# An attention and gated-MLP kernel: score slots, side matmuls and PSUM banks shared between them, and the last block divided on chip

## The chip, the cores and the metric

The kernel runs on one core of a Trainium2 chip. The metric is the device time of one execution in microseconds (us). Every changed kernel here ran four times, with the kernel before beside it on the same chip. Ratios to the kernel before use fast executions alone; medians are over all. The profiled execution of each kernel gives its span, its waits and the clock granted to TensorE (1.0 is full speed). PE is TensorE, PEld its weight loads, DVE VectorE, ACT ScalarE, POOL GpSimd, SP SyncE. "L416" is line 416 of the kernel in question; the line numbers shift a little from one kernel to the next.

## The reference

```python
x  = A_x                                  # 1 x 2048 x 640, bf16
xn = layernorm(x)
q, k, v = split(xn @ wqkv)                # 32 heads of 20
s  = softmax(q @ k.T * 20**-0.5) @ v @ wo
g  = silu((sigmoid(xn @ w_gate) * (xn @ w_up)) @ w_down)   # inner size 1728
return x + s * g
```

The heads are taken four at a time (the four 32-row strips of TensorE's array) and the queries 512 at a time, which makes 8 x 4 = 32 blocks.

## The kernel before

The kernel plans its own issue order. While it is built, a small planner walks through time in steps, holds a model of when each engine is free, and emits one instruction after the other. The chip then executes each engine's list in exactly that order. What waits for what is not the planner's work: the program builder puts in the semaphore waits.

Scores of one key tile and head fill one PSUM bank (128 x 512 fp32). Most are turned into probabilities by an exp on ScalarE, two or three banks in one instruction. Some key tiles go to VectorE, which makes the exponential with integer arithmetic (`iv`, then four passes `pb`). All other matmuls, projections and the MLP, are "side work". These tiles take eight banks of PSUM, the memory that TensorE writes its results to:

```python
SLOT = (3, 2)
scA = [psum.tile([P, n, 512], FP32, name=f"scA{n}", tag=f"scA{n}") for n in SLOT]  # 3 + 2 banks
scD = psum.tile([P, 512], FP32, name="scD", tag="scD")      # scores for VectorE
oacc = psum.tile([P, QC], FP32, name="oacc", tag="oacc")    # sum of values
def misc_ps():                                              # every side matmul
    return psum.tile([P, 512], FP32, tag="misc", bufs=1, name="mps")
...
# ScalarE: one exp over all banks of a slot
exp_act(pt[:, 0:m, :], scA[i][:, 0:m, :])
...
# VectorE: one bank
nc.vector.tensor_scalar(out=d["iv"][:, j, :], in0=scD, scalar1=I_OFF, scalar2=I_LOW, ...)
...
# TensorE: a fill of the slot that is free, plus one head for VectorE, packed side by side
todo = [(scA[nfill % 2][:, x, :],) + t for x, t in enumerate(jobs)]
...; todo.append((scD, dcur["b"], dcur["kt"], js[0]))
```

The packed score matmuls that write a slot are called its fill. A side item, for example a gate tile, takes the one side bank, runs its five matmuls, waits for ScalarE or VectorE to read the bank, and only then gives it to the next.

Of the kernel before, what the change touches and what calls it, by code (L numbers as in the profile page):

```python
# [10 lines left out]
FP32 = mybir.dt.float32  # L11
# [3 lines left out]
ALU = mybir.AluOpType  # L15
# [11 lines left out]
ND = 4  # L27

# [22 lines left out]
def kernel(  # L51
# [50 lines left out]
    ident = const.tile([P, P], BF16, name="ident")  # L102
    esum = const.tile([P, P], BF16, name="esum")
# [30 lines left out]
    mks = {}  # L134
# [8 lines left out]
    def k_max(g, c):  # L143
        if c == 0:
            mks[g] = wk.tile([P, NQC], FP32, tag="mk4", bufs=2, name="mk4")
        nc.vector.tensor_reduce(out=mks[g][:, c:c + 1], in_=kTs[g % 2][:, c * 512:(c + 1) * 512],
                                axis=AXISX, op=ALU.max, apply_absolute_value=True)
        if c == NQC - 1:
            mk = wk.tile([P, 1], FP32, tag="mk", bufs=2, name="mk")
            nc.vector.tensor_reduce(out=mk, in_=mks[g], axis=AXISX, op=ALU.max)  # L150
            nc.vector.tensor_scalar_mul(out=mds[g % 2], in0=esum, scalar1=mk[:, 0:1])
# [41 lines left out]
    with tc.tile_pool(name="ln", bufs=2) as lp, \  # L193
# [10 lines left out]
        make_identity(nc, ident)  # L204
        for w in wqks:
            nc.gpsimd.memset(w.rearrange("p a j e -> p (a j e)"), 0.0)
# [18 lines left out]
        for c in range(NQC):  # L225
# [16 lines left out]
            for i in range(4):  # L242
                if i % 2 == 0:
                    nc.scalar.activation(out=xn[:, i, :], in_=xt[:, i, :], func=ACT.Identity,
                                         bias=nb[:, i, :], scale=rstd[:, i, :])
                else:
                    nc.gpsimd.tensor_scalar(out=xn[:, i, :], in0=xt[:, i, :], scalar1=rstd[:, i, :],
                                            scalar2=nb[:, i, :], op0=ALU.mult, op1=ALU.add)
            for kd in range(KD):
# [5 lines left out]
                if kd % 2 == 0:  # L255
                    nc.scalar.copy(out=dst, in_=tp)
                else:
                    nc.vector.tensor_copy(out=dst, in_=tp)
# [17 lines left out]
    SLOT = (3, 2)  # L276
    scA = [psum.tile([P, n, 512], FP32, name=f"scA{n}", tag=f"scA{n}") for n in SLOT]
    scD = psum.tile([P, 512], FP32, name="scD", tag="scD")
# [3 lines left out]

    def misc_ps():
        return psum.tile([P, 512], FP32, tag="misc", bufs=1, name="mps")
# [19 lines left out]
    LAT = 0.07  # L304
    D_WAIT = 0.0
    T_F, T_PV, T_MM, T_MODE = 0.215, 0.216, 0.216, 0.10
    T_IV, T_PASS, T_ON = 0.655, 0.63, 0.66
    NPT, NPB, NIV = (3, 4), 2, 2

    def t_exp(n):  # L310
        return 0.095 + 0.4267 * n
# [8 lines left out]

    class Item:
        def __init__(self, ops, at, need=None, prio=1):
            self.ops = ops
            self.at = at
            self.need = need
            self.prio = prio
            self.i = 0
            self.ready = 0.0

    def mk_k(g, c, at):  # L330
        st = {}

        def alloc():
# [4 lines left out]
                     ("DVE", 0.66, lambda: k_max(g, c))], at, prio=0)  # L338
# [5 lines left out]
    def mk_q(b, at):  # L344
# [13 lines left out]
        def ev():  # L358
            qs[b] = q_evac(st["ps"])
        return Item([("PE", alloc, [(T_MM, lambda kd=kd: mm(kd)) for kd in range(KD)]),  # L360
                     ("ACT", 0.53, ab),
                     ("PE", None, [(T_MM, lambda: q_bound(st["ps"], g, st["aq"]))]),
                     ("DVE", 0.66, ev, "free", lambda t: q_at.__setitem__(b, t))], at, prio=0)

    def mk_v(pr, tts, at):
# [10 lines left out]
        def done(t):  # L376
            for tt in tts:
                v_at[(pr, tt)] = t + (2.5 if tt in DKT else 0.0)
        nd = sum(tt in DKT for tt in tts)
        return Item([("PE", alloc, [(0.07, lambda i=i, kd=kd: mm(i, kd)) for i in range(len(tts)) for kd in range(KD)]),  # L380
                     ("DVE", 0.1 + 0.18 * len(tts) + 0.28 * nd, lambda: v_evac(st["ps"], pr, tts), "free", done)], at, prio=0)

    def mk_gu(c, kf, at):
# [25 lines left out]
        def ev():  # L409
# [3 lines left out]
                      ("ACT", 0.53, th, "free")], at),  # L413
                Item([("PE", alloc1, [(T_MM, lambda kd=kd: mm("u", 1, kd)) for kd in range(KD)]),
                      ("DVE", 0.66, ev, "free")], at)]

    def mk_down(c, t4, h, at):
# [15 lines left out]
        def ev():  # L433
# [4 lines left out]
        return Item([("PE", alloc, [(0.136, lambda kf=kf: mm(kf)) for kf in range(NFT)]),  # L438
                     ("ACT", 0.37, th), ("DVE", 0.44, ev, "free")], at)

    def mk_out(tt, h, at):
        st = {}

        def alloc():
            if h == 0:
                if not ob:
                    ob.append(late.tile([P, 2, 5 * D], BF16, name="ob", tag="wd"))
                o2 = ob[0][:, tt % 2, :]
                xr, ot = o2[:, 0:D], o2[:, D:2 * D]
                gqr = o2[:, 2 * D:4 * D].bitcast(FP32)  # L450
                nc.sync.dma_start(out=xr, in_=x2[tt * P:(tt + 1) * P, :])
                nc.sync.dma_start(out=gqr, in_=gq_dram[tt * P:(tt + 1) * P, :])
                out_tiles[tt] = (xr, gqr, ot)
            st["ps"] = misc_ps()
# [5 lines left out]
        def ev():  # L460
            xr, gqr, ot = out_tiles[tt]
            sl = slice(h * HD, (h + 1) * HD)
            tmp = ob[0][:, h, 4 * D:5 * D].bitcast(FP32)
# [3 lines left out]
            if h == 1:  # L467
                nc.sync.dma_start(out=out2[tt * P:(tt + 1) * P, :], in_=ot)
        return Item([("PE", alloc, [(0.136, lambda kd=kd: mm(kd)) for kd in range(KD)]),
                     ("DVE", 0.44, ev, "free")], at, need=(NG - 1) * NQC + tt // 4)  # L470
# [9 lines left out]
    nglu = NBLK - NQC  # L480
    gi = 0
    items = [mk_v(0, t, 0.0) for t in VT]
    for b in range(NBLK):
# [7 lines left out]
        if b < nglu:  # L491
            hi = (len(glu) * (b + 1)) // nglu
            mk += glu[gi:hi]
            gi = hi
        elif c > 0:
# [5 lines left out]
        for i, f in enumerate(mk):  # L501
            items += f(b + 0.9 * i / len(mk))

# [3 lines left out]
    claimed = [0]  # L507

    def claim_act(n):
        got = []  # L510
        for b in range(min(NBLK - 1, claimed[0] // NJOB), NBLK):
# [16 lines left out]
    def claim_dve():  # L528
        for b in range(claimed[0] // NJOB, min(NBLK, claimed[0] // NJOB + 2)):
            if d_left[b]:  # L530
# [4 lines left out]
            if a_left[b]:  # L535
                return None
# [12 lines left out]
    pt_left = [[], []]  # L549
# [17 lines left out]
    def pv_emit(us, end):  # L567
        for u in us:
# [15 lines left out]
            left[i][1] = max(left[i][1], end + LAT)  # L584
# [42 lines left out]

    with tc.manual_schedule(engines={ENG.PE, ENG.Activation, ENG.DVE}):
        nc.sync.dma_start(out=wo, in_=A_wo.rearrange("(kd p) e -> p kd e", p=P))
        load_wgu(0, 0)  # L630
# [7 lines left out]
        slots = [dict(full=None, at=0.0), dict(full=None, at=0.0)]  # L638
        nfill, nexp = 0, 0
        dslot = dict(full=None, at=0.0)  # L640
        iv_left = []
        dcur = None
        dve_pass = []
        cur = None
        mode = None
        blk_loaded = -1
        misc_at = 0.0
        extra = []
        norm_pending = None
        STEP = 0.04  # L650

        def progress():
            return claimed[0] / NJOB

        def finish(item, t):
            op = item.ops[item.i]
            item.i += 1
            item.ready = t + LAT
# [3 lines left out]
        while pv_block[0] < NBLK:  # L662
            guard += 1
            assert guard < 60000, ("issue order does not end", now, claimed, pv_block, [len(q) for q in pv_q], slots, dslot, cur and (cur.i, cur.ops[cur.i][0], cur.ready), misc_at, items[:1] and (items[0].at, items[0].need), [(u["b"],u["kt"],u["k"],u["ready"]) for u in pv_q[0][:3]], [(u["b"],u["kt"],u["k"],u["ready"]) for u in pv_q[1][:3]], pt_left[0][-4:], pt_left[1][-4:], pb_left[-3:], iv_left[-3:], dcur and dcur["left"], oacc_at, norm_pending, sorted(v_at)[-3:])
            bb = min(NBLK - 1, claimed[0] // NJOB)
# [7 lines left out]
            if cur is None and misc_at <= now:  # L673
                can = [x for x in items[:80] if x.at <= progress() and (
                    x.need is None or o_at.get(x.need, 1e9) <= now)]
                cur = min(can, key=lambda x: x.prio) if can else None
            if cur is not None and cur in items:
                items.remove(cur)
                cur.ready = now
                step = 0  # L680
            for it in list(extra):
                if it.i >= len(it.ops):
                    extra.remove(it)
            evs = ([cur] if cur is not None else []) + extra


            if free["ACT"] <= now:
                it = next((e for e in evs if e.i < len(e.ops) and e.ops[e.i][0] == "ACT" and e.ready <= now), None)
                s = slots[nexp % 2]
                if it is not None:  # L690
                    op = it.ops[it.i]
                    op[2]()
                    free["ACT"] = now + op[1]
                    finish(it, now + op[1])
                    if len(op) > 3 and op[3] == "free":
                        misc_at = now + op[1] + LAT
                        if it is cur:
                            cur = None
                            if it.i < len(it.ops):
                                extra.append(it)  # L700
                elif s["full"] is not None and s["at"] <= now and buf_free(pt_left[nexp % 2], NPT[nexp % 2]):
                    jobs = s["full"]
                    i = nexp % 2
                    pt = w2.tile([P, SLOT[i], QC], BF16, tag=f"pt{i}", bufs=NPT[i], name=f"pt{i}")
                    m = len(jobs)
                    exp_act(pt[:, 0:m, :], scA[i][:, 0:m, :])
                    end = now + t_exp(m)
                    free["ACT"] = end
                    pt_left[i].append([m, 0.0])
                    for x, (b, kt, j) in enumerate(jobs):  # L710
                        add_unit(b, kt, j, pt[:, x, :], None, end + LAT + 0.1, (pt_left[i], len(pt_left[i]) - 1))
# [209 lines left out]
```

## Time and profile before

The time was 976.27 us (median of 3; 975.0 to 977.9). The profiled execution has a span of 963.7 us. Its own device time was 965.4 us, at a clock of 0.981.

| stage | from, to (us) | what limits it |
|---|---|---|
| head (normalise, transpose, first keys) | 0 to 39.2 | PE waits 18 us for normalised rows |
| attention (first to end of last exp) | 39.2 to 866.8, 827.5 us | ScalarE, closely followed by TensorE |
| tail (last down projections, output) | 866.8 to 963.7, 96.9 us | one PSUM bank, used in turn |

The first lines of the page of the kernel before. Each digit of the middle rows is the busy share of one fortieth of the span, in tenths; PEclk is the granted clock.

```profile
span 963.7 us, 18399 instructions
...
PE 867.8 (90%) x7285; PEld 306.8 (32%) x7372; DVE 768.1 (80%) x1302; ACT 802.9 (83%) x790; POOL 107.3 (11%) x152
...
PE   3799999999999999999999999999999999997664
...
ACT  3769998989999898979999999999999899981000
...
PEclk9799999999999999999999999999999999998889
```

In the attention TensorE is at 9 throughout; ScalarE, from the fourth slice on, is mostly at 9 and else at 8 (once at 7). ScalarE drops to 1 and then to nothing in the last four slices, where TensorE goes on at 7 to 4: that is the tail.

Busy times overlap, so headroom is read from starts. In this timeline of ScalarE (start, duration, what) a three-bank exp (128x1536) is followed 1.33 us later by the next instruction, and a two-bank exp (128x1024) 0.91 us later when nothing is waited for (303.08 to 303.99). After the exp at 300.72 the next one starts 1.02 us later: the other slot was filled late.

```profile
299.39 1.56 ACT L81 ACTIVATE pt_3820<-scA_428 128x1536 bf16<-128x1536 f32 x1
300.72 1.14 ACT L81 ACTIVATE pt_3838<-scA_429 128x1024 bf16<-128x1024 f32 x1
301.74 1.47 ACT L81 ACTIVATE pt_3848<-scA_428 128x1536 bf16<-128x1536 f32 x1
303.08 1.04 ACT L81 ACTIVATE pt_3862<-scA_429 128x1024 bf16<-128x1024 f32 x1
303.99 1.48 ACT L81 ACTIVATE pt_3875<-scA_428 128x1536 bf16<-128x1536 f32 x1
```

By such distances ScalarE needs an estimated 649 of the 700 us between 100 and 800 (93%).

The tail, in the chain of waits (start, duration, what): each down projection (14 matmuls) is followed by a tanh, a multiplication on VectorE, and only then by the next one.

```profile
883.73 2.18 PE mps L425 x14
...
885.93 0.45 ACT td L81
...
886.40 0.50 DVE gqs L435
...
886.95 2.18 PE mps L425 x14
```

Two groups of the view by lines serve for comparison. The columns are: line, engine, operation, out<-in, shapes, count, then busy us and mean ns of one, then idle us just before them with what ended it.

```profile
L747 DVE TENSOR_SCALAR iv<-scD 128x512 int16<-128x512 f32 x452 | 310.0, 686 | 95.4 <-PE scD L540 85.9 <-PE scA_429 L540 5.8 <-PE scA_428 L540 1.5
...
L402 PE MATMUL mps<-xnT,wgu 128*128 128x512 bf16 x465 | 138.4, 383 | 5.6 <-issue 1.3 <-DVE q L168 0.8 <-DVE vf L184 0.8
```

Side matmuls of the MLP hardly ever wait (5.6 us before 465 of them).

### The profile page before, as it was taken

What the parts mean: (1) busy time and instruction counts of PE and PEld (TensorE: products, weight loads), DVE (VectorE), ACT (ScalarE), POOL (GpSimd) and SP (SyncE); (2) the same over time, 40 slices, a digit from 0 to 9 for tenths busy, and PEclk for the clock granted to TensorE, in tenths of its full rate; (3) what the DMA queues carried; (4) which work ended last, traced back from release to release, by engine and by line L of the source; (5) the groups of instructions that cost most, each with busy time, mean ns of one, the idle gap of its engine ahead of it and who ended that gap; (6) DMA issues with size and microseconds to landing.
All of it is one profiled execution on the core that took longest, in us unless ns stands there. A gap on an engine that the chain in (4) does not pass through costs nothing.

```text
span 963.7 us, 18399 instructions
## 1 busy us (share of the span) xinstructions
PE 867.8 (90%) x7285; PEld 306.8 (32%) x7372; DVE 768.1 (80%) x1302; ACT 802.9 (83%) x790; POOL 107.3 (11%) x152
## 2 busy tenths in 40 slices
PE   3799999999999999999999999999999999997664
PEld 1333323333333233332333333333233322223332
DVE  6588889898888888888888889898888888883122
ACT  3769998989999898979999999999999899981000
POOL 4110010110001000100000000110000000000044
PEclk9799999999999999999999999999999999998889
DMA  8301211112110211111110111102121111211366
GB/s 215 126 10 43 49 44 33 47 48 53 30 38 29 52 44 41 45 42 46 45 42 20 41 33 44 44 16 64 44 58 30 38 50 45 62 44 31 109 185 184
DMA packets 85798, 54.53 MB, mean 57 GB/s; under 512 B 33552, under 2 KB 79440, under 8 KB 85712
## 3 DMA queue, kind: packets, MB, share of 16 engines
q1 hardware_dynamic: 84560, 52.05, 19.7%
q8 instruction: 57, 0.93, 0.4%
q10 hardware_dynamic: 1152, 1.31, 0.4%
q14 instruction: 29, 0.24, 0.1%
HBM read 42.32 MB, written 8.39 MB: 53 GB/s over the span
## 4 chain that ended last, share of the span: by engine, by line
PE 49%; ACT 24%; DVE 18%; issue 5%; DMA 3%; POOL 1%; SPq 0%; POOLq 0%; DVEq 0%; another core or an unknown queue 0%; ACTq 0%
PE oacc L580 13%; PE mps L402 10%; DVE pb L625 7%; PE scA_428 L540 6%; PE mps L425 5%; DVE iv L747 5%; PE scA_429 L540 5%; PE scD L540 4%; PE mps L457 2%; PE mps L372 2%; PE mps L341 1%; DVE ob L464 1%; PE mps L352 1%; DMA ob<-gq_dram 1%; DVE hT L410 1%
## 5 line engine op out<-in xcount | busy, mean ns | idle before, releaser
L747 DVE TENSOR_SCALAR iv<-scD 128x512 int16<-128x512 f32 x452 | 310.0, 686 | 95.4 <-PE scD L540 85.9
L625 DVE TENSOR_SCALAR pb<-iv 128x2048 int16<-128x2048 int16 x452 | 307.9, 714 | 3.0
L402 PE MATMUL mps<-xnT,wgu 128*128 128x512 bf16 (+1 forms) x505 | 150.9, 385 | 7.7 <-DVE hT L410 1.4
L610 POOL TENSOR_TENSOR on_bf<-on,rl 128x512 bf16<-128x512 f32 x32 | 42.7, 1335 | 558.0 <-DMA rl<-rd 341.6
L540 PE MATMUL scD<-q,kT_69 32*128 32x512 bf16 x228 | 87.9, 385 | 2.3 <-DVE iv L747 1.8
L425 PE MATMUL mps<-wd,hT 128*128 128x320 bf16 x448 | 80.9, 306 | 8.6 <-DVE gqs L435 7.5
L540 PE MATMUL scD<-q,kT_70 32*128 32x512 bf16 x224 | 85.6, 382 | 2.1 <-DVE iv L747 1.8
L580 PE MATMUL oacc<-pb,vs_74 128*21 128x512 bf16 x684 | 80.2, 382 | 1.7 <-DVE pb L625 1.2
L580 PE MATMUL oacc<-pb,vs_73 128*21 128x512 bf16 x672 | 79.7, 382 | 1.6 <-DVE pb L625 1.3
L540 PEld LDWEIGHTS <-kT_70 32*128 32x128 bf16 x1024 | 38.5, 91 | 123.4 <-issue 119.4
L540 PEld LDWEIGHTS <-kT_69 32*128 32x128 bf16 x1024 | 39.2, 91 | 120.8 <-issue 113.9
L402 PEld LDWEIGHTS <-wgu 128*128 128x128 bf16 (+1 forms) x560 | 44.1, 98 | 85.1 <-issue 58.4
L540 PE MATMUL scA_428<-q,kT_69 32*128 32x512 bf16 x478 | 64.5, 387 | 7.4 <-DVE q L168 3.2
L540 PE MATMUL scA_428<-q,kT_70 32*128 32x512 bf16 x480 | 64.8, 383 | 4.6 <-ACT pt_2941 L81 0.5
L540 PE MATMUL scA_429<-q,kT_70 32*128 32x512 bf16 x320 | 64.0, 383 | 1.4 <-ACT pt_3070 L81 0.4
L540 PE MATMUL scA_429<-q,kT_69 32*128 32x512 bf16 x318 | 63.3, 386 | 1.4 <-ACT pt_7252 L81 0.5
L425 PEld LDWEIGHTS <-hT 128*128 128x128 bf16 x448 | 38.9, 98 | 49.4 <-issue 37.4
L457 PE MATMUL mps<-wo,oU 128*128 128x320 bf16 x160 | 31.2, 332 | 23.1 <-DVE ob L464 22.1
L464 DVE SCALAR_TENSOR_TENSOR ob<-mps,ob 128x320 f32<-128x320 f32 x32 | 15.7, 492 | 38.2 <-PE mps L457 31.1
L81 ACT ACTIVATE tnh<-mps 128x512 bf16<-128x512 f32 (+1 forms) x56 | 35.6, 636 | 10.5 <-PE mps L402 10.5
L410 DVE SCALAR_TENSOR_TENSOR hT<-tnh,mps 128x512 bf16<-128x512 bf16 (+1 forms) x56 | 38.1, 681 | 4.4 <-PE mps L402 3.9
L580 PEld LDWEIGHTS <-v_71 128*21 128x21 bf16 x1024 | 27.7, 90 | 41.1 <-issue 33.0
(1374 smaller groups left out, 1754.5 us busy)
## 6 DMA issues: line engine op xcount, KB each, us to landing
rl<-rd SPq DMA_DIRECT2D x128, 64.0 KB
wgu<-in_B_w_gate_dram SPq DMA_DIRECT2D x24, 320.0 KB
wgu<-in_B_w_up_dram SPq DMA_DIRECT2D x24, 320.0 KB
gq_dram<-gqs SPq DMA_DIRECT2D x32, 160.0 KB
ob<-gq_dram SPq DMA_DIRECT2D x16, 320.0 KB
ob<-in_A_x_dram SPq DMA_DIRECT2D x16, 160.0 KB
out_dram<-ob SPq DMA_DIRECT2D x16, 160.0 KB
oU<-on_bf SPq DMA_DIRECT2D x112, 20.0 KB
```

Of the source, the lines that this page charges most:

```text
L81: return nc.scalar.add_instruction(mybir.InstActivation(func=func, name=nc.get_next_instruction_name(), engine=ENG.Activation, ins=[nc.sca ...
L372: nc.tensor.matmul(st["ps"][:, i * 2 * GC:(i + 1) * 2 * GC], lhsT=xnT[:, kd, tts[i] * P:(tts[i] + 1) * P], rhs=wvs[pr][:, kd, :], start=(k ...
L402: nc.tensor.matmul(st[key][0:fs, :], lhsT=w[:, i, kd, ko * P:ko * P + fs], rhs=xnT[:, kd, c * QC:(c + 1) * QC], start=(kd == 0), stop=(kd ...
L410: nc.vector.scalar_tensor_tensor(out=hT[0:fs, kf, :], in0=st["t"][0:fs, :], scalar=1.0, in1=st["u"][0:fs, :], op0=ALU.add, op1=ALU.mult)
L425: nc.tensor.matmul(st["ps"][:, 0:HD], lhsT=hT[0:fsz[kf], kf, t4 * P:(t4 + 1) * P], rhs=wd[0:fsz[kf], kf, h * HD:(h + 1) * HD], start=(kf = ...
L457: nc.tensor.matmul(st["ps"][:, 0:HD], lhsT=oU[:, kd, tt * P:(tt + 1) * P], rhs=wo[:, kd, h * HD:(h + 1) * HD], start=(kd == 0), stop=(kd = ...
L464: nc.vector.scalar_tensor_tensor(out=tmp, in0=st["ps"][:, 0:HD], scalar=0.25, in1=gqr[:, sl], op0=ALU.mult, op1=ALU.mult)
L540: nc.tensor.matmul(dst, lhsT=kTs[(b // NQC) % 2][32 * j:32 * j + 32, kt * P:(kt + 1) * P], rhs=qs[b][32 * j:32 * j + 32, :], start=True, s ...
L580: nc.tensor.matmul(oacc[32 * j:32 * j + DH + 1, :], lhsT=lhsT, rhs=u["src"], start=first, stop=last, tile_position=(0, 32 * j), skip_group ...
L610: nc.gpsimd.tensor_tensor(out=on_bf, in0=on, in1=rl, op=ALU.mult)
L625: nc.vector.tensor_scalar(out=pb[:, k, :, :].bitcast(I16), in0=iv, scalar1=0.25, scalar2=cst, op0=ALU.mult, op1=ALU.add)
L747: nc.vector.tensor_scalar(out=d["iv"][:, j, :], in0=scD, scalar1=I_OFF, scalar2=I_LOW, op0=ALU.add, op1=ALU.max)
```

## The change

The intent: two score slots of three banks each, of which the third bank is not the slot's own. Together with the bank `mps` these third banks are a pool of three from which an exp, a VectorE score or a side item takes whichever is free. Side work is paced so that it is done when the attention ends. The last block is divided on chip, by transposes, instead of by a trip through DRAM. The head normalises on VectorE.

```diff
-    SLOT = (3, 2)
-    scA = [psum.tile([P, n, 512], FP32, name=f"scA{n}", tag=f"scA{n}") for n in SLOT]
-    scD = psum.tile([P, 512], FP32, name="scD", tag="scD")
+    SLOT = 3
+    scA = [psum.tile([P, SLOT, 512], FP32, name=f"scA{i}", tag=f"scA{i}") for i in range(2)]
...
+    mps = psum.tile([P, 512], FP32, name="mps", tag="mps")
+    bank = [scA[0][:, SLOT - 1, :], scA[1][:, SLOT - 1, :], mps]
+    got_bank = [2]
     def misc_ps():
-        return psum.tile([P, 512], FP32, tag="misc", bufs=1, name="mps")
+        return bank[got_bank[0]]
...
+        def due():     # side work that should be done by now
+            return total * min(1.0, progress() / (NBLK - NQC - 0.2))
...
+                        behind = done < due() + LAG
+                        for f in ((2, (nfill + 1) % 2, nfill % 2) if behind else (2,)):
+                            if flex[f] <= now:
+                                m_bank = f
...
+                    want = SLOT if flex[nfill % 2] <= now and d_bank != nfill % 2 else SLOT - 1
+                    jobs = claim_act(want)
...
+                            score_mm(bank[d_bank], dcur["b"], dcur["kt"], d_new[1])
... (new constants of the planner, items that wait for named events, tail_steps() for the last block,
...  normalisation on VectorE, copies of xnT on ScalarE)
```

## The prediction

> **What bounds it now.** Span 963.7 us, three stages (slices, chain of waits, timeline):
> - Head: the first score matmul starts at 38.75. PE waits 18 us for normalised rows (ScalarE 13.5, GpSimd 4.4).
> - Attention: exps run from 39.2 to 866.8, 827 us for 32 blocks. From 100 to 800 PE is busy 96%, ACT 95%, DVE 87%, but busy times overlap. By start-to-start times ScalarE is tightest: a 3-bank exp takes 1.33, a 2-bank one 0.905, tanh and abs 0.478; it needs 649 of 700 us (93%). 40 of the 51 lost come after the 2-bank exp (mean 1.062): the other slot is filled late. TensorE rounds take 0.22 (four packed matmuls), 0.216 (side), 0.136 (320 columns), plus 0.10 at each change of kind. The Trainium skill, "TensorEngine Tiling (Array Packing)", Key Properties, says that changing the tiling mode drains the engine; the trace agrees (0.32 against 0.216). By the issue order this makes 753 us, 91% of its stage.
> - Tail: 97 us. Eight down projections and 32 output halves share one PSUM bank strictly in turn (3.2 and 1.5 us each), with DMA waits of 3 to 4 us; PE is half idle and its clock falls to 0.5 in places ("TensorE: Matmul & The Clock Gate", Part 1: an idle window throttles it).
>
> **What the change does** (issue order of both).
> - Tail: all downs and 15 halves move into attention. 9 halves remain (about 13 us), then the last block, divided on chip: copy, transposes, 40-odd matmuls, VectorE, output DMA (about 14). Estimate 29 us after the last exp, for 97: minus 68.
> - Head: normalising goes to VectorE (16 ops of about 0.3), all xnT copies to ScalarE: minus 4.
> - Attention: TensorE gets downs (15 us), halves (10), 725 fill rounds for 684; floor 789 for 753. Changes of kind hardly fall (1547 for 1563). ScalarE: 559 2-bank and 166 3-bank exps for 319 and 319, 20 score tiles more: 778 for about 762. VectorE needs about 675, no limit. Against that, side work runs in three banks without its serial wait, and VectorE tiles queue. At ScalarE's old 93% the stage would take 838, at 97% 802. But two engines now need 95% at once, and in most rounds a fill (about 0.7 with latencies) must fit within 0.905, so I expect 94 to 95%: 826 us, as long as before.
>
> **Sum.** 35 + 826 + 29 = 890 us profiled. Timed runs before were 11 above the profiled one (976 for 965), so about 899; I say 896, range 870 to 928. Chances: faster by over 2% 0.94, within 2% 0.05, slower 0.01. The gain comes from tail and head; attention absorbs 36 us of TensorE work at no cost in time.
>
> **What would show it.** Tail: last exp to end about 29 us (right under 36); no chain of down projection, tanh, VectorE. Head: first score near 35, no wait of PE for GpSimd. Attention: exps last about 826; ScalarE's idle per exp falls to about 0.06 (0.157 after 2-bank exps before); VectorE's waits for the score bank (86 us) halve. PE clock 1.0 throughout attention.
>
> **What would make it wrong.** If each 2-bank exp still loses 0.157, attention takes 866 and the time is 935. If the planned order fits the chip's durations very well, 805 and 875. Output halves waiting for rows from DRAM, or for the reciprocal's trip through DRAM, could add 5 to 10 to the tail. If flexible banks make a fill wait for a slow VectorE read, ScalarE starves, as at block changes (waits up to 5 us before).

## The result

The changed kernel takes 1287.56 us (median of 4; 1282.5 to 1300.0) against 975.63 for the kernel before (972.1 to 977.9): 1.322 times as long, with a 95% interval of 1.311 to 1.333. (Ratios are the mean time of one kernel's fast runs over that of the other's of the same rounds, so not quite the ratio of the medians.) Executions over 1.5% slower than the fastest of the same kernel are left out of the means. The output is correct.

The page after:

```profile
span 1298.2 us, 18464 instructions
...
PE 998.7 (77%) x7243; PEld 306.1 (24%) x7328; DVE 757.5 (58%) x1272; ACT 862.8 (66%) x876; POOL 95.3 (7%) x138
...
PE   4777778887877787787887777787877777787775
...
ACT  5567676765556777666678867666657765786760
...
PEclk8589898986678989787799989888879997999888
```

No engine is at 9 anywhere. TensorE, at 7 or 8, is busier in sum than before (998.7 us for 867.8) though it has no more matmuls to do; the clock fell to half in places (0.50 from 40 to 60 us, mean 0.871), and matmuls take longer then.

| us | before | predicted | after |
|---|---|---|---|
| first exp starts | 39.2 | about 35 | 36.7 |
| attention | 827.5 | 826 | 1226.8 |
| tail | 96.9 | 29 | 34.8 |
| span | 963.7 | 890 | 1298.2 |
| idle of ScalarE before exps | 37.5 | | 363.8 |

Head and tail did roughly what was expected. The attention alone lost 400 us. A few microseconds of it, all engines (start, duration, engine, line, what, and in brackets the idle time and what ended it):

```profile
707.99 0.39 PE L560 MATMUL scA_431<-q,kT_69 32*128 32x512 bf16 x2 [0.27 <-DVE iv L843]
...
708.31 0.82 PE L416 MATMUL scA_431<-xnT,wgu 128*128 128x512 bf16 x3
...
709.17 1.02 ACT L83 ACTIVATE pt_6478<-scA_431 128x1024 bf16<-128x1024 f32 x1 [0.43 <-PE scA_431 L416]
710.24 0.38 PE L416 MATMUL scA_431<-xnT,wgu 128*128 128x512 bf16 x1 [1.11 <-ACT pt_6478 L83]
...
710.55 0.39 PE L560 MATMUL scA_430<-q,kT_69 32*128 32x512 bf16 x3
...
710.99 1.45 ACT L83 ACTIVATE pt_6487<-scA_430 128x1536 bf16<-128x1536 f32 x1 [0.80 <-PE mps L560]
```

At 707.99 a fill puts two heads into banks 0 and 1 of the second slot's tile. Then three of five side matmuls go into bank 2 of that tile. The exp reads banks 0 and 1 only (128x1024), and yet it waits 0.43 us for the side matmuls. The fourth side matmul writes bank 2 only, and waits 1.11 us for the exp to end. Behind it in TensorE's list stands the fill for the *other* slot. That slot was free by then (its exp had ended at 708.2, VectorE's read of its third bank at 709.1), but TensorE takes its list in order, so the fill came only at 710.55 and the next exp at 710.99.

The view by lines shows it for the whole run. The same side matmul, by the tile it writes:

```profile
L416 PE MATMUL scA_431<-xnT,wgu 128*128 128x512 bf16 (+1 forms) x186 | 67.5, 423 | 40.7 <-ACT pt_6906 L83 1.6 <-ACT pt_7345 L83 1.5 <-ACT pt_4008 L83 1.3
...
L416 PE MATMUL mps<-xnT,wgu 128*128 128x512 bf16 (+1 forms) x180 | 56.9, 402 | 2.1 <-issue 1.1 <-DVE iv L843 0.4 <-DVE q L172 0.2
...
L416 PE MATMUL scA_430<-xnT,wgu 128*128 128x512 bf16 (+1 forms) x152 | 55.8, 422 | 39.6 <-ACT pt_2089 L83 1.5 <-ACT pt_9793 L83 1.5 <-ACT pt_4471 L83 1.4
```

The 338 that write a third bank of a slot's tile idled 80.3 us before them, the 180 that write the separate tile 2.1 us.

In the built programs I then counted the waits between TensorE, ScalarE and VectorE whose releasing instruction touches the same PSUM tile, but no bank in common:

| kernel | waits on another bank of the same tile |
|---|---|
| before | 0 |
| changed | 1026 |

The Trainium skill, "PSUM — Partial Sum Buffer", section "PSUM bank collisions raise a hardware error", asks for semaphores by bank and quadrant, "by bank is the simple version". The builder here orders by the tile, which is coarser.

### The profile page after: what moved, and what is told of

Same layout as the page of the kernel before. It is cut to its first block, busy times and chain, and to the rows that moved or that the text cites. A ratio compares the mean times of both kernels' runs of the same rounds, so it can differ in the third digit from the quotient of the medians.

```text
span 1298.2 us, 18464 instructions
## 1 busy us (share of the span) xinstructions
PE 998.7 (77%) x7243; PEld 306.1 (24%) x7328; DVE 757.5 (58%) x1272; ACT 862.8 (66%) x876; POOL 95.3 (7%) x138
## 4 chain that ended last, share of the span: by engine, by line
PE 51%; ACT 28%; DVE 15%; issue 4%; DMA 1%; another core or an unknown queue 0%; ACTq 0%; DVEq 0%; SPq 0%; POOL 0%
PE oacc L600 13%; PE scA_430 L560 8%; PE scA_431 L560 8%; DVE iv L843 7%; PE scA_431 L416 4%; PE scA_430 L416 3%; PE scA_430 L439 3%; DVE pb L645 2%; PE mps L416 2%; PE scA_431 L439 2%; PE mps L439 1%; DVE hT L424 1%; PE scA_431 L355 1%; PE scA_431 L366 1%; PE scA_431 L386 1%
## 5 line engine op out<-in xcount | busy, mean ns | idle before, releaser
L645 DVE TENSOR_SCALAR pb<-iv 128x2048 int16<-128x2048 int16 x432 | 292.7, 703 | 2.4
L843 DVE TENSOR_SCALAR iv<-mps 128x512 int16<-128x512 f32 x182 | 124.8, 686 | 114.6 <-PE mps L560 113.3
L843 DVE TENSOR_SCALAR iv<-scA_431 128x512 int16<-128x512 f32 x130 | 89.6, 689 | 129.7 <-PE scA_431 L560 56.7
L843 DVE TENSOR_SCALAR iv<-scA_430 128x512 int16<-128x512 f32 x120 | 82.7, 689 | 108.3 <-PE scA_430 L560 55.6
L560 PE MATMUL scA_431<-q,kT_70 32*128 32x512 bf16 x465 | 93.0, 433 | 16.3 <-DVE iv L843 8.1
L560 PE MATMUL scA_430<-q,kT_70 32*128 32x512 bf16 x468 | 91.7, 435 | 16.4 <-DVE iv L843 7.9
L560 PE MATMUL scA_430<-q,kT_69 32*128 32x512 bf16 x472 | 88.8, 420 | 16.2 <-DVE iv L843 5.5
L560 PEld LDWEIGHTS <-kT_69 32*128 32x128 bf16 x1024 | 41.1, 92 | 248.1 <-issue 245.9
L560 PE MATMUL scA_431<-q,kT_69 32*128 32x512 bf16 x461 | 86.1, 411 | 17.4 <-DVE iv L843 6.8
L416 PE MATMUL scA_431<-xnT,wgu 128*128 128x512 bf16 (+1 forms) x186 | 67.5, 423 | 40.7 <-ACT pt_6906 L83 1.6
L600 PE MATMUL oacc<-pb,vs_74 128*21 128x512 bf16 x684 | 90.3, 433 | 0.5 <-issue 0.5
L416 PE MATMUL scA_430<-xnT,wgu 128*128 128x512 bf16 (+1 forms) x152 | 55.8, 422 | 39.6 <-ACT pt_2089 L83 1.5
L600 PE MATMUL oacc<-pb,vs_73 128*21 128x512 bf16 x612 | 84.0, 440 | 0.5 <-DVE pb L645 0.3
L439 PE MATMUL scA_430<-wd,hT 128*128 128x320 bf16 (+1 forms) x168 | 44.1, 348 | 29.9 <-ACT pt_10955 L83 1.4
L439 PEld LDWEIGHTS <-hT 128*128 128x128 bf16 x448 | 37.5, 101 | 109.3 <-issue 100.0
L416 PE MATMUL mps<-xnT,wgu 128*128 128x512 bf16 (+1 forms) x180 | 56.9, 402 | 2.1 <-issue 1.1
L600 PEld LDWEIGHTS <-v_71 128*21 128x21 bf16 x1024 | 28.9, 95 | 52.1 <-issue 44.6
L560 PE MATMUL mps<-q,kT_70 32*128 32x512 bf16 x91 | 40.1, 441 | 0.0
L600 PEld LDWEIGHTS <-v_72 128*21 128x21 bf16 x1024 | 28.6, 94 | 46.8 <-issue 39.1
```

The lines of the kernel that those rows point to most:

```text
L416: nc.tensor.matmul(st[key][0:fs, :], lhsT=w[:, i, kd, ko * P:ko * P + fs], rhs=xnT[:, kd, c * QC:(c + 1) * QC], start=(kd == 0), stop=(kd ...
L439: nc.tensor.matmul(st["ps"][:, 0:HD], lhsT=hT[0:fsz[kf], kf, t4 * P:(t4 + 1) * P], rhs=wd[0:fsz[kf], kf, h * HD:(h + 1) * HD], start=(kf = ...
L560: nc.tensor.matmul(dst, lhsT=kTs[(b // NQC) % 2][32 * j:32 * j + 32, kt * P:(kt + 1) * P], rhs=qs[b][32 * j:32 * j + 32, :], start=True, s ...
L600: nc.tensor.matmul(oacc[32 * j:32 * j + DH + 1, :], lhsT=lhsT, rhs=u["src"], start=first, stop=last, tile_position=(0, 32 * j), skip_group ...
L645: nc.vector.tensor_scalar(out=pb[:, k, :, :].bitcast(I16), in0=iv, scalar1=0.25, scalar2=cst, op0=ALU.mult, op1=ALU.add)
L843: nc.vector.tensor_scalar(out=d["iv"][:, j, :], in0=bank[bk], scalar1=I_OFF, scalar2=I_LOW, op0=ALU.add, op1=ALU.max)
```

## The experiments

Three theories were open. A: the waits between different banks of one tile cost the time. B: the planned order is too tight for the chip, mostly with exps of only 0.9 us. C: the clock falls for a reason of its own. Runs 1 and 2 are a pair of twins made to part A from the other two.

### 1. Two-bank exps only, third banks still in the slot tile

One exp cannot read two tiles, so the first pair of runs does without three-bank exps. It hardly changes ScalarE's need (estimated 756 us for 779 of the changed kernel, from counts times the distances above, as VectorE takes more tiles).

```diff
-                    want = SLOT if flex[nfill % 2] <= now and d_bank != nfill % 2 else SLOT - 1
+                    want = SLOT - 1
```

> The changed kernel with one edit: a fill never takes the third bank of a slot for scores, so every exp reads two banks; the third banks stay slices of the three-bank slot tiles. Theory A (waits by tile: each access to the third bank waits for the exp or the fill on the other two banks of the same tile, and they for it): still slow, 1230 to 1350 us, as the built program still holds about 1200 waits between accesses to different banks of one tile. Theory B (the planned order is too tight, fills cannot meet exps of 0.9 us): as slow or slower, 1290 to 1400. This run alone does not part them; it is the control of the next one.

Measured: 1395.31 us (1386.7 to 1407.7), ratio to before 1.451, clock 0.845; 1241 waits on another bank. One of the four executions was slow; the three fast ones have a mean of 1392.4. It is 45 us above the range that theory A gave, and inside that of theory B (1290 to 1400), so this run alone would have spoken for B. The waits on another bank rose from 1026 to 1241; the expectation had named about 1200 of them and still put the time too low. Why the same kind of wait cost more here is not shown. The second run of the pair, in which the two theories are far apart, decides. The lines to compare with it:

```profile
span 1386.4 us, 19192 instructions
...
PEclk9678998998888897978897898659879987998966
...
L83 ACT ACTIVATE pt<-scA 128x1024 bf16<-128x1024 f32 x778 | 781.9, 1023 | 448.7 <-PE scA L560 180.5 <-PE scA L416 63.2 <-DVE iv L843 62.7
...
L416 PE MATMUL scA<-xnT,wgu 128*128 128x512 bf16 (+1 forms) x380 | 140.1, 434 | 73.2 <-ACT pt L83 72.0 <-DVE hT L424 0.6 <-DVE gqs L449 0.5
```

### 2. The same order, third banks as tiles of their own

```diff
-    scA = [psum.tile([P, SLOT, 512], ...) for i in range(2)]
+    scA = [psum.tile([P, SLOT - 1, 512], ...) for i in range(2)]
+    third = [psum.tile([P, 512], FP32, name=f"third{i}", tag=f"third{i}") for i in range(2)]
-    bank = [scA[0][:, SLOT - 1, :], scA[1][:, SLOT - 1, :], mps]
+    bank = [third[0], third[1], mps]
```

On TensorE, ScalarE and VectorE every instruction has the same place, operation and operands but for the names of the PSUM tiles.

> The same issue order as the run before (instruction by instruction on TensorE, ScalarE and VectorE), but the two third banks are PSUM tiles of their own. Theory A: the waits between banks are gone, the attention part takes what the prediction said, 810 to 850 us, the whole 860 to 920, and the clock is above 0.97. Theory B (order too tight) and theory C (the clock falls for a reason of its own, for example many short matmuls): still above 1200 us, clock below 0.92.

Measured: 932.65 us (929.3 to 936.4), ratio to before 0.971 (0.963 to 0.979), 463 us below its twin (460 between the means of the fast runs); no wait on another bank; clock 0.989; correct output. Its page and groups:

```profile
span 927.6 us, 19250 instructions
...
PE 876.6 (94%) x7508; PEld 290.0 (31%) x7508; DVE 809.6 (87%) x1392; ACT 805.2 (87%) x929; POOL 101.0 (11%) x138
...
PE   3799999999999999999999999999999999999965
...
ACT  3699999999999989899999999899998999999810
...
PEclk9799999999999999999999999999999999999998
```

```profile
L83 ACT ACTIVATE pt<-scA 128x1024 bf16<-128x1024 f32 x778 | 749.2, 1037 | 60.6 <-PE scA L561 24.0 <-PE mps L561 17.1 <-PE third L561 14.2
...
L417 PE MATMUL third<-xnT,wgu 128*128 128x512 bf16 (+1 forms) x380 | 114.6, 384 | 0.7 <-DVE iv L844 0.4
...
L417 PE MATMUL mps<-xnT,wgu 128*128 128x512 bf16 (+1 forms) x180 | 55.2, 384 | 1.1 <-DVE iv L844 0.9
```

The idle time of the side matmuls is gone (0.7 us before 380, where the twin had 73.2). Before 778 exps ScalarE idles 60.6 us in all, where the twin had 448.7. Theory A stands. B falls, as the order is the same. C falls as well: with the waits gone the clock is back, so its fall was a consequence. How much of the 400 us the half clock itself added on top of the waits, these runs do not separate. The clock records in the trace of the changed kernel allow an estimate. In its attention the clock was at full for 908 us, in which ScalarE took up 1310 banks of scores (0.69 us each), and at half for 319 us, in which it took up 306 (1.04 us each); the kernel before took 0.52 us per bank at full clock. At the pace of the full clock all 1616 banks would take about 1120 us, so roughly 107 of the 399 us go with the half clock, and 292 are there without it. Which rounds fell into the slow stretches was not up to chance, so this stays an estimate.

The whole is 13 us over the range that I gave. The attention took 846.3 us, inside what I expected for it (810 to 850); the tail took 43.6 us, as more output halves were left for it: 86 of their matmuls, five each, so about 17 halves, stand after the last value matmul in its list, against 9 to 10 halves in the changed kernel.

### 3. The kernel before, its order unchanged, with one bank merged into a slot's tile

The reverse test: give the kernel before the same kind of waits.

```diff
+    scA3 = psum.tile([P, 3, 512], FP32, name="scA3", tag="scA3")
+    scA2 = psum.tile([P, 3, 512], FP32, name="scA2", tag="scA2")
+    scA = [scA3, scA2[:, 0:2, :]]
+    scD = scA2[:, 2, :]                 # run 3a: the VectorE scores
     # or, run 3b, with scD left alone:
     def misc_ps():
+        return scA2[:, 2, :]            # the side matmuls
```

> The kernel before with its order unchanged, and only the PSUM bank of the VectorE scores made the third bank of the tile of the two-bank slot. Theory A: the built program gains about 860 waits between different banks of one tile, and the time rises by 15 to 35 per cent, to 1100 to 1300 us. Theories B and C: no change, 970 to 985 us, since the order is the same and every bank is used as before.

> The counterpart of the run in which only the VectorE score bank of the kernel before was merged into the tile of the two-bank slot (1217 us): here only the bank of the side matmuls is merged, the order again unchanged. Theory A: 736 waits between different banks of one tile, slower too. Each side item holds the bank for several matmuls and an exp on that slot must wait for them, so about as much as the other: 1100 to 1300 us. If side matmuls were harmless and only the VectorE scores mattered, under 1020 us.

Measured: 1217.25 us for the VectorE scores (1202.2 to 1232.2, two of the four slow; fast mean 1205.5; ratio 1.254; 865 such waits; clock 0.951) and 1311.45 for the side matmuls (1294.2 to 1312.5; ratio 1.341; 736 waits; clock 0.882). In both programs every instruction stands where it stood before. So either kind of sharing alone is costly in a kernel whose order was good: 243 us (between the means of fast runs) and 337 us, where the changed kernel lost 312. In 3a the clock stayed at 0.951, so most of that loss is the waits themselves. The 736 waits cost more than the 865, so the number of waits does not give the loss. The side run lies 11 us above its range. Groups by line, run 3a:

```profile
L81 ACT ACTIVATE pt<-scA 128x1024 bf16<-128x1024 f32 x319 | 327.1, 1025 | 176.8 <-DVE iv L749 117.9 <-PE scA L542 56.6 <-DVE pb L627 0.4
...
L749 DVE TENSOR_SCALAR iv<-scA 128x512 int16<-128x512 f32 x452 | 311.6, 689 | 312.6 <-PE scA L542 200.8 <-ACT pt L81 109.9 <-ACT tnh L81 0.3
```

and run 3b:

```profile
L81 ACT ACTIVATE pt<-scA 128x1024 bf16<-128x1024 f32 x319 | 326.3, 1023 | 161.8 <-PE scA L404 53.6 <-PE scA L427 21.5 <-PE scA L354 13.9
...
L404 PE MATMUL scA<-xnT,wgu 128*128 128x512 bf16 x520 | 160.3, 402 | 77.9 <-ACT pt L81 70.1 <-DVE hT L412 2.7 <-DVE q L168 1.6
```

In 3a the two-bank exps wait 117.9 us for VectorE's reading of the third bank, and VectorE idles 312.6 us before its reads (95.4 before). In 3b the two-bank exps wait for three kinds of side matmul, and the side matmuls of the MLP wait 70.1 us for exps.

### 4. The plan of the change, with tiles of their own

Is the plan of the changed kernel any worse than the two-bank one? Here its order is kept on TensorE and VectorE, instruction by instruction; ScalarE issues each three-bank exp as two.

```diff
-                            exp_act(pt[:, 0:m, :], scA[nexp % 2][:, 0:m, :])
+                            exp_act(pt[:, 0:min(m, 2), :], scA[nexp % 2][:, 0:min(m, 2), :])
+                            if m == SLOT:
+                                exp_act(pt[:, 2, :], third[nexp % 2])
...
-                            score_mm(scA[nfill % 2][:, x, :], *t)
+                            score_mm(scA[nfill % 2][:, x, :] if x < 2 else third[nfill % 2], *t)
```

> The changed kernel with its own planned order (TensorE and VectorE instruction by instruction the same), but with the third banks as PSUM tiles of their own; since one exp cannot read two tiles, each of the 166 three-bank exps is issued as a two-bank and a one-bank exp (1.383 for 1.33 us, about 9 us in all). Theory A: the whole 390 us excess of the attention goes; from floors of 787 us for TensorE and 788 for ScalarE, at the 94 per cent that the two-bank kernel with own tiles reached, the attention takes about 838, the whole 905 to 930 us. If part of the excess came from the plan itself, the time stays above 960.

Measured: 921.35 us (920.9 to 921.8), ratio 0.953 (0.944 to 0.962), clock 0.989, one wait on another bank left. First exp at 38.0, attention 847.8, tail 34.1. The plan was sound: 366 us came with the tiles, and with the split of the three-bank exps that they ask for (the pair of runs 1 and 2 is the one in which nothing but the tiles differs). The attention is 10 us over my figure of 838: by the estimates both engines are used to 93% of it (787 and 788 of 847.8), not 94.

### 5. The tail, the head and one planner constant

Three banks instead of one for the output halves after the attention, first on the two-bank kernel, then on that of run 4:

```diff
-                        behind = done < due() + LAG
+                        behind = done < due() + LAG or pv_block[0] >= NBLK
```

> The two-bank kernel with own tiles, and one edit: once the last block's values are summed, side matmuls may use all three banks instead of one. The output halves after the attention took 1.49 us each, one at a time; with three banks the wait for VectorE goes: 0.6 us less each, 5 to 9 us less in all than the kernel it is made from (932.7), 922 to 929 us.

> Both edits together: the changed kernel's plan with own tiles and split exps, and three banks for the last output halves. Expected 5 to 8 us under the run with split exps alone, 897 to 924 us, and the fastest of all so far.

Measured: 925.78 us (924.7 to 927.3), 6.9 below its parent (measured in another round, on another chip; the tail in the profiles is 37.3 us for 43.6), as expected; and 919.63 (918.0 to 919.9), only 1.7 below its parent for an expected 5 to 8. The latter is the fastest kernel, ratio to before 0.951 (0.941 to 0.962). In the profiles its tail is 4.5 us shorter than its parent's (29.6 for 34.1), but the attention took 850.2 for 847.8, with the order unchanged. The timeline of VectorE in the tail shows one thing that was lost: the halves now come so fast that one waits 3.90 us for its rows from DRAM.

```profile
893.46 0.49 DVE L484 SCALAR_TENSOR_TENSOR ob<-mps,ob 128x320 f32<-128x320 f32 x1 [0.26 <-POOL ob L486]
894.36 1.09 DVE L484 SCALAR_TENSOR_TENSOR ob<-third,ob 128x320 f32<-128x320 f32 x2 [0.41 <-DMA ob<-gq_dram]
899.35 0.49 DVE L484 SCALAR_TENSOR_TENSOR ob<-mps,ob 128x320 f32<-128x320 f32 x1 [3.90 <-DMA ob<-gq_dram]
```

In the changed kernel the same halves came at a steady 1.49 us, one bank in turn:

```profile
1266.88 0.49 DVE L483 SCALAR_TENSOR_TENSOR ob<-mps,ob 128x320 f32<-128x320 f32 x1 [0.18 <-issue]
1268.38 0.49 DVE L483 SCALAR_TENSOR_TENSOR ob<-mps,ob 128x320 f32<-128x320 f32 x1 [1.00 <-PE mps L476]
1269.86 0.49 DVE L483 SCALAR_TENSOR_TENSOR ob<-mps,ob 128x320 f32<-128x320 f32 x1 [0.99 <-PE mps L476]
```

The fastest kernel with the old head:

```diff
-                nc.vector.tensor_scalar(out=xn[:, i, :], in0=xt[:, i, :], ...)
+                (rows alternately on ScalarE and GpSimd; copies of xnT alternately on ScalarE and VectorE)
```

> The fastest version so far (own tiles, split exps, three banks in the tail: 919.6 us) with the head of the kernel before: rows normalised on ScalarE and GpSimd, copies of xnT shared by ScalarE and VectorE. The prediction said 4 us for the head; the first score matmul came at 36.0 against 38.8. Expected 2 to 4 us slower, 921 to 924 us, and the first score near 38.8.

Measured: 922.0 us (920.8 to 923.0), 2.4 more, first score at 37.9 for 36.0. But the two kernels ran in different rounds on different chips, and among the runs with the new head the first score came between 36.0 and 37.7. So a gain from the new head is not shown.

The fastest kernel, with the planner told to break a running series later for a fill:

```diff
-URGENT, ROUNDS, HOLD, ... = 0.15, 3, 0.15, ...
+URGENT, ROUNDS, HOLD, ... = -0.1, 3, 0.15, ...
```

> The fastest version with one number of its planner changed, so that a running series of side or value matmuls is broken later for a fill (1407 changes of kind on TensorE for 1547). TensorE's floor falls by 11 us, from 787 to 776, but fills come later, nearer to the end of the exp before. If TensorE's changes of kind are what bounds it now, 908 to 916 us; if ScalarE waiting for fills is, 920 to 950.

Measured: 927.73 us (926.6 to 928.5), 8 more (again in another round, on another chip), in the second of the ranges given. The attention took 862.5 us for 850.2, but ScalarE's idle time before exps hardly changed (41.0 us for 41.1), so that the exps' supply got worse is not shown. Part of it is moved work: 7 output halves instead of 10 were left for the tail, which took 24.3 us for 29.6. Saving changes of kind on TensorE did not pay here; where those 8 us come from stays open.

## Why the prediction was wrong

It said 896 us (870 to 928) and the chip said 1287.6.

- **The step that failed: "side work runs in three banks without its serial wait, and VectorE tiles queue."** It counted three free banks where the program had two tiles, each ordered as one thing. The serial wait was not removed but spread: now the exp, the side item and the VectorE score of a slot wait for each other. ScalarE idled 363.8 us before exps where it had idled 37.5, and the attention took 1226.8 us for the predicted 826. The 366 us between the changed kernel and run 4, which has the same order on TensorE and VectorE, is that step's price; runs 1 and 2 price it at 460 us (fast runs) with not one instruction in another place.
- The warnings did not name it. "If flexible banks make a fill wait for a slow VectorE read" came nearest, but spoke of a bank that is in use; the waits here are for banks that nobody uses. The built program was at hand before the prediction and held the 1026 waits.
- "Attention 826 us at 94 to 95%": wrong in size even without those waits. Run 4 took 847.8, of which about 9 us are its split exps (an estimate: ScalarE needs 788 us for 779, at 93%); both engines stayed at 93%, ScalarE's figure from before. Less these 9 us it comes to about 839, the 838 that the prediction itself gave for 93%.
- "PE clock 1.0 throughout attention": 0.871 over the run; 0.989 in run 4. It follows the waits. The trace adds that no long pause was needed: between 60 and 1250 us TensorE never idled longer than 1.65 us before a matmul, and yet the clock fell to 0.5 again and again, 36 times within the attention.
- "Tail 29 us": 34.8, right by its own mark of 36. The ten remaining halves took 1.49 us each and began only when the last values were summed. The saving, 62 us of the 68 expected, is real, as run 4 shows (34.1).
- "First score near 35, no wait of PE for GpSimd": 36.0, and no such wait; TensorE waits 14.7 us for VectorE's rows instead of 18 for those of ScalarE and GpSimd.
- The 11 us between timed and profiled runs, from which the figure was raised, are no cost of timing but two levels of the kernel before. In the three later rounds 6 of its 23 executions took 959.6 to 964.5 us at a clock of 0.981 to 0.989, and 17 took 972.0 to 980.6 us at 0.952 to 0.968. The profiled execution (965.4 us, 0.981) belongs to the first kind, the three timed ones (975.0 to 977.9 us), by their time, to the second. In run 4 the profiled execution took 921.6 us and the median was 921.4. Against the 6 executions at the high clock (mean 961.9) run 4 is 4.2% faster; the ratios given for runs 4 and 5 mix both levels.

## What to carry to other kernels

Here the program builder ordered two users of one PSUM tile even when they touched different banks: give every bank that is lent out separately a tile of its own, and split an instruction that would span two tiles, which here cost about 9 us (estimated) and left a gain of 366. Before trusting a planned order, count in the built program the waits whose two sides have no bank in common; that needs no chip. When a change is expected to remove a wait and every engine's busy share falls instead, look for a pair of lines in the timeline that wait for each other without sharing data.

## What the Trainium skill lacked or had wrong

- "PSUM — Partial Sum Buffer" tells to guard by bank, but not that banks inside one tile may be ordered together by the builder, nor what that costs: 1395.3 against 932.7 us for the same instruction order. I found it on none of the pages.
- "TensorEngine Tiling (Array Packing)", Key Properties, says that a change of tiling mode drains the engine, without a figure: here a change of kind (from a fill to a side matmul, 707.99 to 708.31 in the timeline of the result) took about 0.32 us from start to start, against 0.216 without one.
